# A jump, two branch hints and marker loads on TensorE's way through a decode kernel

## The chip, the cores and the metric

The kernel runs on one core of a Trainium2 chip. The time is device microseconds of one execution; the numbers given for a kernel are the median of several runs, with the lowest and the highest. The engines are named as in the profile: PE (TensorE matmuls), PEld (TensorE's weight loads), DVE (VectorE), ACT (ScalarE), POOL (GpSimd) and SP (SyncE), and beside them 16 DMA engines that move data between HBM and the on-chip memory.

## What is computed

One token (a row `x` of 1024) goes through a layer norm, and then through an attention block over a cached window and an MLP, side by side; both are added to `x`. Cut to what matters:

```python
def _A_ref(x, k_cache, v_cache, wq, wo):        # Hq 32, Hkv 4, Sk 65536, Dh 128
    W = min(4096, max(256, Sk // 4))            # 4096 last positions
    q = (x @ wq).reshape(B, Sq, Hq, Dh).transpose(0, 2, 1, 3)
    k = jnp.repeat(k_cache[:, :, Sk - W:, :], rep, axis=1)
    v = jnp.repeat(v_cache[:, :, Sk - W:, :], rep, axis=1)
    p = _softmax(jnp.einsum("bhqd,bhkd->bhqk", q, k) * (Dh ** -0.5))
    o = jnp.einsum("bhqk,bhkd->bhqd", p, v)
    return o.transpose(0, 2, 1, 3).reshape(B, Sq, Hq * Dh) @ wo

def _B_ref(x, w1, b1, w2, b2):                  # D 1024, F 3584
    h = _gelu(_layernorm(x) @ w1 + b1)
    return h @ w2 + b2

xn = _layernorm(x)
return x + _A_ref(xn, k_cache, v_cache, wq, wo) + _B_ref(xn, w1, b1, w2, b2)
```

All tensors are bfloat16.

## The kernel before

The kernel is written engine by engine, with every order and every semaphore set by hand. Nearly all of its traffic is weights and cache, each byte of which is used once.

**The loads.** SP issues all large loads on one queue, in this order: W1 (line 158, `load_rows`), the first four of each partition's eight rows of Wq (line 158), the other four (lines 229 and 230), two K loads and two V loads (line 237, `load_cache`), W2 (line 158) and Wo in four chunks of 20, 10, 1 and 1 rows (line 158, `WO_CHUNKS`). W2 is loaded into the place of W1, and Wo into that of Wq, so W2 is issued after the W1 matmuls (`C["h"]`) and Wo after the Wq matmuls (`C["q"]`); V waits for the bias matmuls (`C["b1"]`), whose row lies where V goes. ACT issues three small loads at the start: the row `x`, `b1` and `b2`.

**The detour of part of Wq.** A partition `p` holds the rows `8p` to `8p+7` of Wq. The last 1024 columns (`CUT`) of the last row of each odd partition aren't loaded into their place. Line 229 loads the even partitions whole, line 230 the odd ones without those 2 KB, and line 233 loads the 64 missing pieces with four DMAs of 16 rows into `WX`, a corner of `Pb` that is needed only later. The hole in `WA` and `WX` are set to zero first by POOL (lines 169 and 170), for which SP waits (`C["hole"]`). The q row is then made of the matmuls of line 345, which use a masked copy `XNZ7` of the normed x for the cut columns, and of four further matmuls (line 354) on `WX` with `XEZ`. `XPR`, `XEZ`, `XNZ7` and `EVEN` serve only this.

**The work on PE, in order.** The row `x` is turned into a column (lines 262 and 266), the sums for two layer norms are made (275 and 299), the bias row is put into PSUM (315). Then come the W1 matmuls (324), the Wq matmuls (345 and 354), 128 transposes of K (405), the scores (431), the transposes of the MLP's row (438), a few small matmuls for the softmax, P times V (510), and the output rows, which gather W2 (494), and after the attention's row is normed, Wo (494). Five matmuls with unused results (543, `KEEP_BUSY`) stand behind the first chunk of Wo. ACT copies the result (547), SP stores it.

**The instructions of PE.** They lie in one straight run, with no branch. Each matmul is a weight load and a matmul instruction, 763 of each in the profile. They aren't all on the engine at the start: in the trace a DMA queue of its own, q8, brings blocks of 16 KB during the run.

Of the kernel before, what the change touches and what calls it, by code (L numbers as in the profile page):

```python
# [5 lines left out]
ALU = mybir.AluOpType  # L6
ACTF = mybir.ActivationFunctionType
AX = mybir.AxisListType
# [11 lines left out]
KC = D // 128  # L20
NQ = HQ * DH
WQ_CHUNKS = [4, 4]
W1_CHUNKS = [8]
W2_CHUNKS = [28]
WO_CHUNKS = [20, 10, 1, 1]
KEEP_BUSY = [[512] * 5, [], [], []]
NPAIR = HKV // 2
PB = 2 * NBLK
CUT = 1024
B1W = 256  # L30
B1N = F // B1W
XS = 2
XROWS = 48
# [16 lines left out]
def bass_parallel_sum__sliding_block_cached__mixer_channel_mlp__decode_kernel(  # L50
# [22 lines left out]

    s_xrow, s_b1, s_b2, s_out = (nc.alloc_semaphore(n) for n in ("s_xrow", "s_b1", "s_b2", "s_out"))
    s_wq = sems("s_wq", len(WQ_CHUNKS))
    s_ex = nc.alloc_semaphore("s_ex")
# [11 lines left out]
    def sb(name, shape, d):  # L88
        return nc.alloc_sbuf_tensor(name, shape, d)
# [16 lines left out]
    EVEN = sb("EVEN", [128, 1], f32)  # L106
    XNZ7 = sb("XNZ7", [128, 15], bf16)
    XPR = sb("XPR", [1, XS * XROWS], bf16)
    XEZ = sb("XEZ", [XROWS, XS * 15], bf16)
# [28 lines left out]
    WX = Pb[0:XROWS, 0:XS * CUT]  # L138
# [7 lines left out]
    wq_runs = A_wq.rearrange("(p r) n -> p (r n)", r=KC)  # L146
    wq_x = A_wq.rearrange("(s h r e k) n -> k s h e r n", s=XS, h=2, r=4, e=4)[2 * KC - 1]
# [4 lines left out]

    C = {}

# [13 lines left out]

    POOL.mark(pool.memset(WA[:, KC * NQ - CUT:KC * NQ], 0.0))
    C["hole"] = POOL.mark(pool.memset(WX, 0.0))  # L170
    POOL.mark(pool.memset(XPR[:, :], 0.0))
# [7 lines left out]
    pool.wait_ge(s_xrow, 16)  # L179
    for i in range(XS):  # L180
        at = i * 2 * 16 * 2 * KC
        dst = XPR[0:1, i * XROWS:(i + 1) * XROWS].rearrange("o (g m) -> o g m", g=3)[:, 0:3:2, :]
        C["xpr"] = POOL.mark(pool.tensor_copy(
            dst.rearrange("o h (e r) -> o h e r", e=4),
            XBR[0:1, at + 2 * KC - 1:at + 2 * 16 * 2 * KC:2 * KC].rearrange("o (h r e) -> o h e r", h=2, e=4)))
# [5 lines left out]
    POOL.mark(pool.memset(XNZ[:, :], 0.0))  # L191
    POOL.mark(pool.memset(XNZ7[:, :], 0.0))
    C["xnz"] = POOL.mark(pool.memset(XEZ[:, :], 0.0))
# [32 lines left out]
    load_rows(WA, wq_p, WQ_CHUNKS[:-1], NQ, s_wq)  # L226
    sp.wait_ge(POOL.sem, C["hole"])
    c0 = (KC - WQ_CHUNKS[-1]) * NQ
    sp.dma_start(WA[0:128:2, c0:KC * NQ], wq_runs[0:128:2, c0:KC * NQ]).then_inc(s_wq[-1], 16)
    sp.dma_start(WA[1:128:2, c0:KC * NQ - CUT], wq_runs[1:128:2, c0:KC * NQ - CUT]).then_inc(s_wq[-1], 16)  # L230
    for i in range(XS):
        for h in range(2):
            sp.dma_start(WX[32 * h:32 * h + 16, i * CUT:(i + 1) * CUT], wq_x[i, h, :, :, NQ - CUT:NQ]).then_inc(s_ex, 16)

# [22 lines left out]

    xt = PS[:, 7 * 512 + 16: 7 * 512 + 24]
# [4 lines left out]
    xe = PS[0:XROWS, 7 * 512 + 24: 7 * 512 + 24 + XS]  # L263
    pe.wait_ge(POOL.sem, C["xpr"])
    for i in range(XS):
        last = pe.matmul(xe[:, i:i + 1], lhsT=XPR[0:1, i * XROWS:(i + 1) * XROWS], rhs=oneb[0:1, :])
# [17 lines left out]
                               op0=ALU.subtract, op1=ALU.mult))  # L284
    dve.wait_ge(POOL.sem, C["xnz"])
    DVE.mark(dve.tensor_scalar(out=XEZ[:, 7:XS * 15:15], in0=xe, scalar1=msx[0:XROWS, 2:3], scalar2=msx[0:XROWS, 7:8],
                               op0=ALU.subtract, op1=ALU.mult))
    C["even"] = DVE.mark(dve.tensor_reduce(out=EVEN[:, 0:1], in_=identf[:, 0:128:2], axis=AX.X, op=ALU.add))
    dve.wait_ge(DVE.sem, DVE.cnt)
    C["xn"] = DVE.mark(dve.tensor_copy(XNTb[:, :], XNT[:, :]))  # L290
    pool.wait_ge(DVE.sem, C["xn"])
    C["xnz7"] = POOL.mark(pool.tensor_tensor(out=XNZ7[:, 7:8], in0=XNTb[:, KC - 1:KC], in1=EVEN[:, 0:1], op=ALU.mult))
# [12 lines left out]
    ACT.mark(act.activation(out=EXPW[:, 0:1], in_=msy[:, 6:7], func=ACTF.Exp))  # L305
    dve.wait_ge(ACT.sem, C["std2"])
# [12 lines left out]
    k = 0  # L319
    for j, n in enumerate(W1_CHUNKS):  # L320
        pe.wait_ge(s_w1[j], 16)
        for _ in range(n):
            for t in range(7):
                last = pe.matmul(  # L324
                    PS[0:1, t * 512:(t + 1) * 512], lhsT=YTb[:, k:k + 1],
                    rhs=W1[:, k * F + t * 512: k * F + (t + 1) * 512],
                    start=False, stop=(k == KC - 1))
            k += 1
# [7 lines left out]
    k = 0  # L336
    for j, n in enumerate(WQ_CHUNKS):
        pe.wait_ge(s_wq[j], 16 if j < len(WQ_CHUNKS) - 1 else 32)
        for _ in range(n):
            for t in range(8):  # L340
                cut = k == KC - 1 and (t + 1) * 512 > NQ - CUT
                if cut:
                    pe.wait_ge(POOL.sem, C["xnz7"])
                z = XNZ7[:, 7 - t:15 - t] if cut else XNZ[:, 15 * k + 7 - t:15 * k + 15 - t]
                pe.matmul(  # L345
                    PS[0:8, 7 * 512:8 * 512], lhsT=z,
                    rhs=WA[:, k * NQ + t * 512: k * NQ + (t + 1) * 512],
                    start=(k == 0 and t == 0), stop=False)
            k += 1
    pe.wait_ge(s_ex, 32 * XS)  # L350
    for i in range(XS):
        for t in range((NQ - CUT) // 512, 8):
            at = i * CUT + t * 512 - (NQ - CUT)
            last = pe.matmul(  # L354
                PS[0:8, 7 * 512:8 * 512], lhsT=XEZ[:, 15 * i + 7 - t:15 * i + 15 - t], rhs=WX[:, at:at + 512],
                start=False, stop=(i == XS - 1 and t == 7))
# [34 lines left out]
    for u in range(NUNIT):  # L391
        banks = KPAIRS[u % 3]
        if u == 2:
            turn_q()
        if u == 0:
            pe.wait_ge(ACT.sem, C["a_hrow"])
            pe.wait_ge(DVE.sem, C["d_hrow"])
        if u >= 3:
            wait_kt(pe, u - 3)
        if u % 4 == 0:  # L400
            pe.wait_ge(s_k[u // 4], 16)
        col = u * 2048
        for bb in range(16):
            o = banks[bb // 8] * 1024 + (bb % 8) * 128
            last = pe.matmul(PSb[:, o:o + 128], lhsT=KT[:, col + bb * 128: col + (bb + 1) * 128],  # L405
                             rhs=identb[:, :], is_transpose=True)
        C["ktr"][u] = PE.mark(last)
        use_act = u not in (2, 5)
        dve.wait_ge(PE.sem, C["ktr"][u])
        for s in range(1 if use_act else 2):  # L410
            bk = banks[s]
            C["dkt"][u] = DVE.mark(dve.tensor_copy(  # L412
                KT[:, col + 1024 * s: col + 1024 * (s + 1)], PSb[:, bk * 1024:(bk + 1) * 1024]))
        if use_act:
            bk = banks[1]
            act.wait_ge(PE.sem, C["ktr"][u])
            C["akt"][u] = ACT.mark(act.activation(  # L417
                out=KT[:, col + 1024: col + 2048], in_=PSb[:, bk * 1024:(bk + 1) * 1024], func=ACTF.Copy))
# [7 lines left out]
    for i in range(NPAIR):  # L426
        for b in range(PB):
            if i == NPAIR - 1 and b == 3 * PB // 4:
                wait_kt(pe, 7)
            o = b * HQ + i * 2 * REP  # L430
            last = pe.matmul(  # L431
                PS[:, o:o + 2 * REP], lhsT=KT[:, (i * PB + b) * 128:(i * PB + b + 1) * 128],
                rhs=QT[:, i * 2 * REP:(i + 1) * 2 * REP],
                start=False, stop=(i == NPAIR - 1 and b % 16 == 15))
    C["sc"] = PE.mark(last)
    pe.wait_ge(DVE.sem, C["d_QT"])
    for c in range(FC):
        last = pe.matmul(PSb[:, 7 * 1024 + 2 * c: 7 * 1024 + 2 * c + 1], lhsT=Hrow[0:1, c:F:FC],
                         rhs=identb[0:1, 0:1], is_transpose=True)
    C["hT"] = PE.mark(last)  # L440
# [28 lines left out]
    C["d_T"] = DVE.mark(dve.tensor_tensor(out=U2[:, :], in0=U2[:, :], in1=HT[:, :], op=ALU.mult))  # L469
    act.wait_ge(DVE.sem, C["se"])  # L470
# [18 lines left out]
    def out_rows_mms(weights, vec, chunks, semaphores, j, stop_at=None):  # L489
        c0 = sum(chunks[:j])  # L490
        pe.wait_ge(semaphores[j], 16)
        for c in range(c0, c0 + chunks[j]):
            for a in range(4):
                ins = pe.matmul(acc(a), lhsT=vec[:, c:c + 32],  # L494
                                rhs=weights[:, c * D + a * 256: c * D + (a + 1) * 256],
                                start=False, stop=(c == stop_at))
        return ins
# [11 lines left out]
    for b in range(PB):  # L509
        last = pe.matmul(PS[0:32, 4 * 512:4 * 512 + NPAIR * DH], lhsT=Pb[:, b * HQ:(b + 1) * HQ], rhs=V4[:, :, b, :],  # L510
                         start=(b == 0), stop=(b == PB - 1))
    C["pv"] = PE.mark(last)
# [68 lines left out]
```

## The time and the profile before

| what | value |
|---|---|
| time, median of 3 runs (lowest to highest) | 100.59 us (100.56 to 101.07) |
| span of the profiled execution | 99.4 us (the page's rounding; 99.35 in the trace) |
| time less span | 1.24 us |
| busy: PE, PEld, DVE, ACT, POOL | 69.6, 42.4, 25.8, 12.8, 9.0 us |
| SP's queue q1: packets, moved, share of 16 engines' span | 1832, 39.85 MB, 94.1% |
| instruction queue q8: packets, moved | 6, 0.10 MB |
| ACT's queue q10: packets, moved | 32, 0.01 MB |
| mean rate over the span | 402 GB/s |

The profiled execution's own time isn't listed apart from its span; the time less the span stands for what lies around it.

The page's second part cuts the span into 40 slices, with the busy share of each engine and of the DMA engines in tenths. The fourth part follows the chain of waits back from the last instruction. The timeline lists the instructions by their start, merged where they follow one another; in brackets stands how long the engine was idle before and what ended it. The third part parts the DMA traffic by queue: q1 is SP's, q10 is ACT's, q8 is TensorE's instructions.

### The profile page before, as it was taken

What the parts mean: (1) busy time and instruction counts of PE and PEld (TensorE: products, weight loads), DVE (VectorE), ACT (ScalarE), POOL (GpSimd) and SP (SyncE); (2) the same over time, 40 slices, a digit from 0 to 9 for tenths busy, and PEclk for the clock granted to TensorE, in tenths of its full rate; (3) what the DMA queues carried; (4) which work ended last, traced back from release to release, by engine and by line L of the source; (5) the groups of instructions that cost most, each with busy time, mean ns of one, the idle gap of its engine ahead of it and who ended that gap; (6) DMA issues with size and microseconds to landing.
All of it is one profiled execution on the core that took longest, in us unless ns stands there. A gap on an engine that the chain in (4) does not pass through costs nothing.

```text
span 99.4 us, 1681 instructions
## 1 busy us (share of the span) xinstructions
PE 69.6 (70%) x763; PEld 42.4 (43%) x763; DVE 25.8 (26%) x50; ACT 12.8 (13%) x15; POOL 9.0 (9%) x30
## 2 busy tenths in 40 slices
PE   0230860089999999999999999722799995009961
PEld 0220300023434343434399869510567894008740
DVE  0058500000000090000078921867790040000000
ACT  0500240000000050000065730005200000000001
POOL 7989100000000000000000000000000000000000
PEclk9999999999999999999999999555557999855799
DMA  9988889999999999999999999998999899699930
GB/s 347 392 372 369 370 369 485 465 422 422 422 422 422 409 402 403 441 429 442 429 429 422 429 534 416 468 485 369 392 485 425 346 445 528 287 404 437 405 143 1
DMA packets 1870, 39.96 MB, mean 402 GB/s; under 512 B 244, under 2 KB 262, under 8 KB 584
## 3 DMA queue, kind: packets, MB, share of 16 engines
q1 hardware_dynamic: 1832, 39.85, 94.1%
q8 instruction: 6, 0.10, 0.4%
q10 hardware_dynamic: 32, 0.01, 0.0%
HBM read 39.86 MB, written 0.00 MB: 401 GB/s over the span
## 4 chain that ended last, share of the span: by engine, by line
DMA 65%; PE 31%; ACT 0%; SPq 0%; issue 0%
DMA WA<-in_A_wo_dram 46%; DMA W<-in_B_w_dram 19%; PE PS L324 15%; PE PS L345 14%; PE PS L494 2%; PE PS L354 1%; ACT ORow L547 0%; SPq L158 0%
## 5 line engine op out<-in xcount | busy, mean ns | idle before, releaser
L324 PE MATMUL PS<-W,YTb 128*1 128x512 bf16 x56 | 14.4, 425 | 6.2 <-DMA W<-in_B_w_dram 6.2
L345 PE MATMUL PS<-WA,XNZ 128*8 128x512 bf16 x64 | 14.0, 379 | 0.0
L324 PEld LDWEIGHTS PS<-W,YTb 128*1 128x1 bf16 x56 | 5.1, 91 | 16.0 <-issue 10.3
L510 PE MATMUL PS<-KV,Pb 128*32 128x256 bf16 x64 | 10.0, 333 | 1.2 <-ACT Pb L471 1.2
L494 PE MATMUL PS<-WA,OT 128*32 128x256 bf16 x128 | 5.6, 345 | 7.1 <-DMA WA<-in_A_wo_dram 7.1
L345 PEld LDWEIGHTS PS<-WA,XNZ 128*8 128x8 bf16 x64 | 5.6, 88 | 8.2
L510 PEld LDWEIGHTS PS<-KV,Pb 128*32 128x32 bf16 x64 | 7.4, 118 | 3.9 <-ACT Pb L471 1.7
L494 PEld LDWEIGHTS PS<-WA,OT 128*32 128x32 bf16 x128 | 4.5, 123 | 8.4 <-issue 6.3
L333 DVE CAST ROW<-PS 1x2048 bf16<-1x2048 f32 x1 | 2.3, 2279 | 22.2 <-PE PS L324 22.2
L417 ACT ACTIVATE KV<-PS 128x1024 bf16<-128x1024 bf16 x6 | 5.8, 1021 | 16.1 <-PE PS L405 16.1
L405 PE MATMUL PS<-identb,KV 128*128 128x128 bf16 x128 | 7.5, 219 | 0.0
L405 PEld LDWEIGHTS PS<-identb,KV 128*128 128x128 bf16 x128 | 7.2, 98 | 0.5 <-issue 0.4
L412 DVE COPY KV<-PS 128x1024 bf16<-128x1024 bf16 x10 | 6.4, 686 | 1.1 <-PE PS L405 1.1
L331 ACT ACTIVATE ROW<-PS 1x1536 bf16<-1x1536 f32 x1 | 1.4, 1440 | 21.2 <-PE PS L324 21.2
L359 DVE CAST Q<-PS 8x512 bf16<-8x512 f32 x1 | 0.7, 678 | 12.5 <-PE PS L354 12.5
L475 DVE TENSOR_REDUCE SUMP<-Pb 128x32 f32<-128x2048 bf16 x1 | 3.6, 3566 | 1.2 <-ACT Pb L471 1.2
L547 ACT ACTIVATE ORow<-PS 128x256 bf16<-128x256 f32 x1 | 0.4, 384 | 27.0 <-PE PS L494 27.0
L299 PE MATMUL PS<-YT,onesf 128*128 128x16 f32 x2 | 0.6, 383 | 4.2 <-DVE YT L297 4.2
L431 PEld LDWEIGHTS PS<-QT,KV 128*128 128x128 bf16 x128 | 3.3, 96 | 0.4 <-issue 0.4
L494 PE MATMUL PS<-W,GT 128*32 128x256 bf16 x112 | 3.4, 273 | 0.0
L431 PE MATMUL PS<-QT,KV 128*128 128x16 bf16 x128 | 3.4, 169 | 0.0
L442 DVE TENSOR_REDUCE MXP<-PS 128x32 f32<-128x2048 f32 x1 | 2.3, 2292 | 3.9 <-PE PS L431 3.9
(104 smaller groups left out, 48.8 us busy)
## 6 DMA issues: line engine op xcount, KB each, us to landing
W<-in_B_w_dram SPq DMA_DIRECT2D x2, 7168.0 KB, 31.0
WA<-in_A_wo_dram SPq DMA_DIRECT2D x1, 5120.0 KB, 40.0
WA<-in_A_wq_dram SPq DMA_DIRECT2D x1, 4096.0 KB, 28.6
KV<-in_A_k_cache_dram SPq DMA_DIRECT2D x2, 2048.0 KB, 40.2
KV<-in_A_v_cache_dram SPq DMA_DIRECT2D x2, 2048.0 KB, 43.6
WA<-in_A_wo_dram SPq DMA_DIRECT2D x1, 2560.0 KB, 45.7
WA<-in_A_wq_dram SPq DMA_DIRECT2D x1, 2048.0 KB, 31.2
WA<-in_A_wq_dram SPq DMA_DIRECT2D x1, 1920.0 KB, 36.7
```

The source lines that it names most:

```text
L324: last = pe.matmul(PS[0:1, t * 512:(t + 1) * 512], lhsT=YTb[:, k:k + 1], rhs=W1[:, k * F + t * 512: k * F + (t + 1) * 512], start=False, s ...
L331: C["a_hrow"] = ACT.mark(act.activation(out=Hrow[:, 0:1536], in_=PS[0:1, 0:1536], func=ACTF.Copy))
L333: C["d_hrow"] = DVE.mark(dve.tensor_copy(Hrow[:, 1536:F], PS[0:1, 1536:F]))
L345: pe.matmul(PS[0:8, 7 * 512:8 * 512], lhsT=z, rhs=WA[:, k * NQ + t * 512: k * NQ + (t + 1) * 512], start=(k == 0 and t == 0), stop=False)
L405: last = pe.matmul(PSb[:, o:o + 128], lhsT=KT[:, col + bb * 128: col + (bb + 1) * 128], rhs=identb[:, :], is_transpose=True)
L412: C["dkt"][u] = DVE.mark(dve.tensor_copy(KT[:, col + 1024 * s: col + 1024 * (s + 1)], PSb[:, bk * 1024:(bk + 1) * 1024]))
L417: C["akt"][u] = ACT.mark(act.activation(out=KT[:, col + 1024: col + 2048], in_=PSb[:, bk * 1024:(bk + 1) * 1024], func=ACTF.Copy))
L431: last = pe.matmul(PS[:, o:o + 2 * REP], lhsT=KT[:, (i * PB + b) * 128:(i * PB + b + 1) * 128], rhs=QT[:, i * 2 * REP:(i + 1) * 2 * REP], ...
L442: C["mxp"] = DVE.mark(dve.tensor_reduce(out=MXP[:, :], in_=PS[:, 0:2048].rearrange("p (b n) -> p n b", b=PB), axis=AX.X, op=ALU.max))
L475: C["sump"] = DVE.mark(dve.tensor_reduce(out=SUMP[:, :], in_=Pb[:, :].rearrange("p (b n) -> p n b", b=PB), axis=AX.X, op=ALU.add))
L494: ins = pe.matmul(acc(a), lhsT=vec[:, c:c + 32], rhs=weights[:, c * D + a * 256: c * D + (a + 1) * 256], start=False, stop=(c == stop_at))
L510: last = pe.matmul(PS[0:32, 4 * 512:4 * 512 + NPAIR * DH], lhsT=Pb[:, b * HQ:(b + 1) * HQ], rhs=V4[:, :, b, :], start=(b == 0), stop=(b == ...
```

## The change

Three things come, and one goes.

- **A jump at TensorE's start.** Its first instruction is a hint, which names a later branch and where that leads; then it jumps to `L_1`. The stub `L_1` stands far down, between two groups of K transposes: a no-op and a branch to `L_main`, behind the jump. The straight run jumps over the stub (`L_after`) when it gets there.
- **A second hint** among the score matmuls, for a branch some 90 instructions further on, to `L_main` again. That branch compares a register that holds 0 with 0 and is never taken. `count` in the loops finds the places, given by `BLOCK_AT`.
- **Marker loads.** ACT issues 15 DMAs behind its `EXPW` activation: load n moves n rows of 2n elements from `x` into a corner of `Pb`. Nothing reads them. The softmax's Exp, which writes `Pb`, waits for them.
- **The detour of Wq goes**, with the zeroing, the masked copies and the extra matmuls. Wq is loaded in two DMAs of four rows, all by `load_rows`.

TensorE's program has the same number of instructions before and after, since six matmuls and their weight loads go and the jumps, hints and labels come.

The diff, cut to its core:

```diff
+BLOCK_AT = [450, 640, 730]
-CUT = 1024
-XS = 2
-XROWS = 48
...
+    def at_block(i):
+        if i == 1:
+            pe.br("L_after")
+            nc.switch_bb("L_1", parent=None)
+            pe.nop(hint="t")
+            pe.br("L_main").branch_hint(first[0])
+            nc.switch_bb("L_after", parent=None)
+        if i == 2:
+            first.append(pe.mark_branch_hint_location())
+        if i == 3:
+            pe.br_lt(zero, 0, on_true="L_main", on_false="S_3").branch_hint(first[-1])
+            nc.switch_bb("S_3")
...
+    def count(n=2):
+        done[0] += n
+        if places and done[0] >= places[0]:
+            places.pop(0)
+            at_block(len(BLOCK_AT) - len(places))
...
-    POOL.mark(pool.memset(WA[:, KC * NQ - CUT:KC * NQ], 0.0))
-    C["hole"] = POOL.mark(pool.memset(WX, 0.0))
...
-    load_rows(WA, wq_p, WQ_CHUNKS[:-1], NQ, s_wq)
-    sp.wait_ge(POOL.sem, C["hole"])
-    c0 = (KC - WQ_CHUNKS[-1]) * NQ
-    sp.dma_start(WA[0:128:2, c0:KC * NQ], wq_runs[0:128:2, c0:KC * NQ]).then_inc(s_wq[-1], 16)
-    sp.dma_start(WA[1:128:2, c0:KC * NQ - CUT], wq_runs[1:128:2, c0:KC * NQ - CUT]).then_inc(s_wq[-1], 16)
-    for i in range(XS):
-        for h in range(2):
-            sp.dma_start(WX[32 * h:32 * h + 16, i * CUT:(i + 1) * CUT], wq_x[i, h, :, :, NQ - CUT:NQ]).then_inc(s_ex, 16)
+    load_rows(WA, wq_p, WQ_CHUNKS, NQ, s_wq)
...
+    first.append(pe.mark_branch_hint_location())
+    pe.br("L_1")
+    nc.switch_bb("L_main", parent=None)
+    pe.reg_mov(zero, 0)
...
+    for n in range(1, 16):
+        act.dma_start(Pb[64:64 + n, 32 * n:32 * n + 2 * n], A_x.rearrange("b s (k n) -> (b s k) n", n=64)[0:n, 0:2 * n]).then_inc(s_mark, 16)
...
-    pe.wait_ge(s_ex, 32 * XS)
-    for i in range(XS):
-        for t in range((NQ - CUT) // 512, 8):
-            at = i * CUT + t * 512 - (NQ - CUT)
-            last = pe.matmul(
-                PS[0:8, 7 * 512:8 * 512], lhsT=XEZ[:, 15 * i + 7 - t:15 * i + 15 - t], rhs=WX[:, at:at + 512],
-                start=False, stop=(i == XS - 1 and t == 7))
...
+    act.wait_ge(s_mark, 16 * 15)
```

## The prediction

> **What bounds the kernel now.** I read the page's DMA rows first, then the chain of waits, then the timeline of the two ends.
>
> ```profile
> span 99.4 us, 1681 instructions
> PE 69.6 (70%) x763; PEld 42.4 (43%) x763; DVE 25.8 (26%) x50; ACT 12.8 (13%) x15; POOL 9.0 (9%) x30
> ...
> DMA  9988889999999999999999999998999899699930
> ...
> q1 hardware_dynamic: 1832, 39.85, 94.1%
> q8 instruction: 6, 0.10, 0.4%
> q10 hardware_dynamic: 32, 0.01, 0.0%
> ```
>
> PE is busy for 70% of the span, but queue q1, which is SP's, keeps 16 DMA engines busy for 94% of it. The row by slices has no hole until the end. Note q8: six transfers of 0.10 MB together, which are blocks of instructions.
>
> ```profile
> 49.89 45.70 DMA WA<-in_A_wo_dram
> 95.59 0.04 issue
> 95.64 1.61 PE PS L494 x48
> 97.24 0.02 issue
> 97.26 0.38 ACT ORow L547
> ```
>
> This is the end of the chain of waits: the last load of Wo, then 48 small matmuls, one copy, the store. Of the 45.70 us almost all is queueing behind older loads.
>
> ```profile
> 89.61 4.00 PE L494 MATMUL PS<-WA,OT 128*32 128x256 bf16 x80 [6.18 <-DMA WA<-in_A_wo_dram]
> ...
> 95.64 1.57 PE L494 MATMUL PS<-WA,OT 128*32 128x256 bf16 x48 [0.96 <-DMA WA<-in_A_wo_dram]
> 96.92 0.10 PEld L494 LDWEIGHTS PS<-WA,OT 128*32 128x32 bf16 x4 [0.18 <-DMA WA<-in_A_wo_dram]
> ```
>
> In the timeline of the end PE stands idle for 6.18 us before the first Wo chunk, and again before the later ones. So PE has some 6 us to give away, and the time is set by the moment when the slowest of the 16 DMA engines is done.
>
> The page doesn't part the engines, but the trace's packet records (start, duration, size) do. Each engine is strictly serial: its next packet starts 3 to 4 ns before the recorded end of the last. So the packets join into 16 chains, each of which must follow the program's order of loads. This gives the last landing of every engine:
>
> - 7 plain engines: 94.37 to 94.85 us.
> - 4 engines that carry sixteen 2 KB packets more (the four WX loads of L233; all of them fall on the same four engines): 95.81 to 96.12 us.
> - 5 engines that carry one 16 KB instruction block each (q8 at 36.59, 56.24, 64.49, 75.15 and 85.86 us): 96.06, 96.38, 96.11, 96.21 and 96.26 us. The sixth block, at 96.75, comes after the data.
>
> So a fetch of TensorE's own code sets the end: 96.38 us. From there to the end of the span are 2.97 us of tail. The span is 99.35 us unrounded, the median of the runs 100.59; I carry the difference of 1.24 us along, so a microsecond on the last engine is a microsecond of the result.
>
> **The change, part by part.**
>
> *The WX detour goes.* Before, each engine loads four packets of 30,720 bytes (1,138 ns) for the odd partitions; after, it is 32,768 bytes (1,213 ns): 4 x 75 = +0.30 us on all 16 engines, less one 4-byte semaphore packet (9 ns): +0.29. The four WX engines lose 16 x 84 + 4 x 9 = 1.38 us, but they weren't last. The five fetch engines are, and they get only the +0.29. With it go two and four matmuls of PE, three DVE and POOL steps and two POOL memsets (2.75 us) ahead of `oneb`; none of this is on the path, since y is ready at 12.6 us and W1 lands at 20.2. SP loses its wait for POOL and four issues, but it only fills a queue that has a backlog.
>
> *Fetches that stay.* Of a fetch I take the price from its own engine: between two landings that the neighbours pass in equal time, an engine with a fetch needs 1.44 to 1.55 us more (0.93 to 1.04 us for the packet, the rest in slower neighbours). Take the fetch (about 1.5) or the WX packets (1.38) off each chain, and the engines' own ends lie from 94.37 to 94.88, mean 94.65. After the change: mean 94.95, plus 1.5 where a fetch falls. With about five engines hit, the latest should again stand near the upper end, at 96.65.
>
> *Marker loads.* Load n has n rows. In the trace of before a DMA of 14 rows leaves 14 packets, one to an engine, and one of a single row leaves one; so load n should use n engines, the lowest one all 15 times and the sixteenth never. A marker is below the 512-byte packets (25 to 27 ns) and above the 4-byte ones (9 ns), with a semaphore packet of 9 ns behind it: 18 to 36 ns, or 0.27 to 0.54 us on the first engine and near nothing on the last. The fetch engines weren't the first four: at most 11 markers, 0.20 to 0.40. I take 0.1, as for an engine in the upper half. On ACT the 15 issues cost 0.43 to 0.85 us each by its three issues of before, together 6 to 13 us:
>
> ```profile
> 12.28 0.29 DVE L309 TENSOR_SCALAR YTb<-YT,msy 128x8 bf16<-128x8 f32 x1
> ...
> 13.36 0.20 ACT L305 ACTIVATE EXPW<-msy 128x1 f32<-128x1 f32 x1
> ...
> 34.75 1.44 ACT L331 ACTIVATE ROW<-PS 1x1536 bf16<-1x1536 f32 x1 [21.18 <-PE PS L324]
> ```
>
> They stand behind EXPW, and ACT's next work waited 21.18 us for PE: covered, and uncovered only beyond 21 us. The new wait on `s_mark` ahead of the softmax's Exp (68.24 us) is long fulfilled.
>
> *The jump.* TensorE jumps into its third 16 KB block of instructions, runs a no-op and jumps back. No branch is in the trace. Below, it costs nothing (both blocks at hand); above, a fetch each way, each 1.0 us plus a wait behind a packet of W1 (57,344 bytes, 2.1 to 2.8 us): about 8 us. PE's first matmul was at 3.71 us; later PE stands idle 6.21 us for W1, and again 6.18 us for Wo. I take 4 us, hidden. On the DMA engines it adds one to three fetches in the first 8 us. The first may run before W1's first packet (1.81 us) and cost nearly nothing; the others cost 1.5 us, on engines that have no other fetch, as long as each fetch goes to another engine, which is what the five of before did.
>
> *The second hint.* It announces a branch back to the first block that is never taken: one more fetch, or the fetch of the next block comes late. From nothing to 1.5 us on one engine, and a wait of up to 4 us for PE near 75 us, before the idle 6.18. I take one fetch on an engine of its own: no price.
>
> [...] The rows show five fetches on five engines. [...]
>
> Sum: 0.29 + 0.1 = +0.39 us, 100.98: **101.0 us**.
>
> **Rivals.**
>
> 1. *One engine gets two fetches: slower.* With the stub, its way back and the second hint, the fetches beside the data rise from five towards nine. If the order of engines comes round again by then (five are known to differ, no more), an engine ends at 94.95 + 3.0 = 97.95 instead of 96.65: about 102.3. If the first of the two is the early one, half hidden before W1, about 101.5. It decides from the first doubled engine on. For it: the count rises. Against it: up to 16 engines are free. Chance 0.34.
> 2. *The fetches beside the data go away: faster.* If the early visit left later blocks in place, so that no engine has one, the end is at 94.88 + 0.29 = 95.17, 1.2 us earlier: 99.4. But one stub visits one block, and a single fetch left holds the end at 96.2 or later. Chance 0.10. [...]
> 3. *TensorE becomes the bound.* The jump's return and a late block after the wrong hint together exceed the idle 6.18 us. It takes over 7 us of stall: 101.5 to 104. Chance 0.06.
> 4. *The hints do nothing* (all at hand, no further fetch): the sum is the same +0.39, so it is part of the forecast.
>
> **How the numbers follow.** Forecast 0.50. Its own range, from the engines' spread (0.25) and the markers (0 to 0.4), is 100.6 to 101.2; 0.5% of 100.59 is 0.5 us, about what a measurement of this kernel can tell from no change, so of this 0.50, 0.37 is the same, 0.11 slower, 0.02 faster. Rival 1 (0.34) and 3 (0.06) are slower, rival 2 (0.10) faster. Slower 0.51, same 0.37, faster 0.12. The range reaches from 100.5 up to the doubled engine with markers, 102.5, and leaves out rival 2, the worst of rival 3 and some of the edges.
>
> **What would show it.** Right: q1 with the same 39.85 MB, q8 with seven to eleven blocks, one to three of them before 10 us; the 2 KB packets between Wq and K gone; the plain engines ending 0.3 us later; the last engine with one fetch, near 96.7, and the tail still 3.0 us. Wrong: an engine with two fetches; no q8 block between 30 and 90 us; PE not idle before the first Wo chunk; a gap in q1.

## The result, and the profile after

The changed kernel takes 101.09 us (median of 16 runs, 100.86 to 101.33), against 100.68 us for the kernel before, timed beside it in 16 runs. The ratio is 1.0042 with a 95% interval from 1.0033 to 1.0051: some 0.42 us slower. The profiled execution took 101.11 us; its span is 99.76 us, so 1.35 us lie around it.

From the page of the changed kernel, its first rows, the DMA busy share by slices, and the queues (packets, MB, share of 16 engines' span):

```profile
span 99.8 us, 1679 instructions
PE 68.5 (69%) x757; PEld 42.1 (42%) x757; DVE 24.2 (24%) x48; ACT 12.8 (13%) x15; POOL 5.6 (6%) x22
...
DMA  9988899899999999999999999999889699799920
...
q1 hardware_dynamic: 1736, 39.85, 93.7%
q8 instruction: 6, 0.10, 0.4%
q10 hardware_dynamic: 272, 0.02, 0.2%
```

The 39.85 MB of q1 are the same. It has 96 packets fewer: the 64 WX pieces of 2 KB and 32 semaphore packets. q10 has the 240 packets of the markers. q8 still has six blocks, which is the first surprise. TensorE's profiled instructions are 1,542 against 1,546 before, four fewer and not the same number: twelve matmuls and weight loads went, and eight branches, hints and the like came. That didn't decide the blocks, since experiment 1 below, with 1,534, has six as well.

The end of the chain of waits, in order of time:

```profile
50.80 45.23 DMA WA<-in_A_wo_dram
96.03 0.04 issue
96.07 1.55 PE PS L482 x48
97.62 0.02 issue
97.65 0.38 ACT ORow L537
```

It is the same chain, 0.4 us later. From the timeline, PE before Wo and ahead of the last matmuls:

```profile
90.05 4.46 PE L482 MATMUL PS<-WA,OT 128*32 128x256 bf16 x80 [6.67 <-DMA WA<-in_A_wo_dram]
...
96.07 1.33 PEld L482 LDWEIGHTS PS<-WA,OT 128*32 128x32 bf16 x48 [0.61 <-DMA WA<-in_A_wo_dram]
96.07 1.52 PE L482 MATMUL PS<-WA,OT 128*32 128x256 bf16 x48
```

PE again stands idle for 6.67 us before the first chunk of Wo, so it isn't the bound. Joining the packet records into 16 serial chains, as the prediction did, gives the last landing of each engine:

| engines | before | after |
|---|---|---|
| plain | 7: 94.37 to 94.85 us | 11: 94.88 to 95.41 |
| with the WX pieces | 4: 95.81 to 96.12 | none |
| with one instruction block beside the data | 5: 96.06 to 96.38 | 5: 96.51, 96.54, 96.59, 96.62, 96.77 |

The markers give the engines their numbers: in the trace load n has n packets of 4n bytes, from 1 of 4 bytes to 15 of 60, and the engine whose chain carries the last 15 - e of the loads is called e (engine 0 has all). In the changed kernel the engine of the first block is number 5. The start of each block, in us from the start of the span:

| kernel | q8 blocks |
|---|---|
| before | 36.59, 56.24, 64.49, 75.15, 85.86, 96.75 |
| after | 2.63, 56.95, 64.88, 77.04, 86.04, 97.15 |

The jump moved the first of the six from 36.59 to 2.63 us and added none.

### The profile page after: what moved, and what is told of

It is laid out like the page before. It is cut to its first block, busy times and chain, and to the rows that moved or that the text cites. A ratio compares the mean times of both kernels' runs of the same rounds, so it can differ in the third digit from the quotient of the medians.

```text
span 99.8 us, 1679 instructions
## 1 busy us (share of the span) xinstructions
PE 68.5 (69%) x757; PEld 42.1 (42%) x757; DVE 24.2 (24%) x48; ACT 12.8 (13%) x15; POOL 5.6 (6%) x22
## 3 DMA queue, kind: packets, MB, share of 16 engines
q1 hardware_dynamic: 1736, 39.85, 93.7%
## 4 chain that ended last, share of the span: by engine, by line
DMA 66%; PE 30%; ACT 0%; issue 0%; SPq 0%
DMA WA<-in_A_wo_dram 45%; DMA W<-in_B_w_dram 21%; PE PS L317 15%; PE PS L335 14%; PE PS L482 2%; ACT ORow L537 0%; SPq L173 0%
## 5 line engine op out<-in xcount | busy, mean ns | idle before, releaser
L499 PE MATMUL PS<-KV,Pb 128*32 128x256 bf16 x64 | 8.8, 310 | 1.3 <-ACT Pb L459 1.3
L262 PE MATMUL PS<-oneb,XBR 1*128 1x1 bf16 x8 | 0.6, 196 | 5.5 <-POOL OUTM L213 5.5
L308 PE MATMUL PS<-KV,oneb 1*1 1x512 bf16 x7 | 3.1, 620 | 0.5 <-DMA KV<-in_B_b_dram 0.5
```

The lines of the kernel that those rows point to most:

```text
L308: last = pe.matmul(PS[0:1, t * 512:(t + 1) * 512], lhsT=oneb[64:65, :], rhs=B1R[:, 2 * t:2 * t + 2, :], start=True, stop=False)
```

## The experiments

Ratios are to the kernel before, timed beside each changed version, with the 95% interval. Two ratios of different experiments that are 0.1 to 0.2% apart are at the edge of what their intervals can part.

### What each part of the change costs

**1. The detour alone** (`x1_detour_only`):

```diff
-BLOCK_AT = [450, 640, 730]
+BLOCK_AT = []
-    pe.br("L_1")            # with its hint and label
-    for n in range(1, 16):  # the marker loads
-        act.dma_start(Pb[64:64 + n, ...
-    act.wait_ge(s_mark, 16 * 15)
```

> The changed kernel without jump, hints and markers: of the change only the removal of the Wq detour is left. Theory (every engine loads 8 KB more, and the engines with a fetch of TensorE code are last): +0.29 us on the kernel before, so about 100.97, q8 with six blocks, the first near 36 us. Rival (the detour cost nothing, the whole +0.41 comes from jump and hints): 100.7, as before.

Measured: 1.0026 (1.0015 to 1.0037), 100.98 us. So 0.26 us of the 0.42 come from the detour's removal. The q8 blocks stand at 37.00, 55.88, 62.74, 75.54, 84.57 and 97.40 us; plain engines end at 94.75 to 95.28 us, those with a block at 96.34 to 96.93.

**2. Without the markers** (`x2_no_markers`): only the last three lines of the diff above.

> The changed kernel without the 15 marker loads and the wait for them. Theory (a marker costs 18 to 36 ns on each engine it uses, the fetch engines carry 5 to 10 of them): 0.1 to 0.2 us faster than the changed kernel, 100.9 to 101.0, the same as the removal of the detour alone. Rival (markers fit into gaps of the queue): 101.09, no difference.

Measured: 1.0024 (1.0012 to 1.0035), 101.06 us; 0.18% below the changed kernel's ratio, a difference good to some 0.15%, and no different from experiment 1.

**3. Without jump and hints** (`x3_no_jump`): only the first lines of that diff, markers kept.

> The changed kernel without jump, stub and both hints, markers kept. Theory (the jump only moves the fetch of the third block from 36 us to 2.6 us, and a fetch costs its engine 1.5 us wherever it stands): the same as the changed kernel, 101.05 to 101.15, with W1 landing 1.2 us earlier and TensorE's W1 matmuls starting near 20.4 instead of 21.9 us. Rival (the early fetch delays all that follows): 0.3 us or more faster.

Measured: 1.0038 (1.0026 to 1.0050), 101.13 us: the changed kernel's 1.0042 again, within some 0.15%. The timelines of this kernel and then of the changed one show what the jump does, at PE's first matmul and at its first W1 matmul:

```profile
2.24 0.63 PE L258 MATMUL PS<-oneb,XBR 1*128 1x1 bf16 x8 [2.24 <-DMA XBR<-in_A_x_dram]
...
20.50 2.72 PE L313 MATMUL PS<-W,YTb 128*1 128x512 bf16 x6 [7.75 <-DMA W<-in_B_w_dram]
```

```profile
5.51 0.63 PE L262 MATMUL PS<-oneb,XBR 1*128 1x1 bf16 x8 [5.51 <-POOL OUTM L213]
...
21.87 1.44 PE L317 MATMUL PS<-W,YTb 128*1 128x512 bf16 x3 [7.78 <-DMA W<-in_B_w_dram]
```

PE starts 3.3 us later and gets W1 1.4 us later. (The POOL named in the bracket is only what ended last by the profile; `oneb` was set at 0.90 us.) Nothing of it reaches the end, since PE waits for Wo later. W1 is late because the block is fetched on one of the 16 engines that bring W1, whose first W1 packet starts at 3.50 us instead of 1.8 to 2.5.

**4. The kernel before, with markers** (`x4_before_marked`):

```diff
+    for n in range(1, 16):
+        act.dma_start(Pb[64:64 + n, 32 * n:32 * n + 2 * n], A_x...[0:n, 0:2 * n]).then_inc(s_mark, 16)
...
+    act.wait_ge(s_mark, 16 * 15)
     act.wait_ge(DVE.sem, C["se"])
```

> The kernel before with the 15 marker loads added, nothing else. Theory: +0.1 to +0.2 us, 100.8 to 100.9. The markers name the engines: the four with the sixteen 2 KB packets are 0 to 3, the five with a fetch lie above them. Rival (markers are free): 100.7.

Measured: 1.0018 (1.0008 to 1.0028), 100.91 us. The markers cost about as much as on the changed kernel. The four WX engines are numbers 0 to 3, by their markers, and the first block falls on number 5, as in the changed kernel and in experiment 3. I don't give the numbers of the later blocks' engines: where two engines end within a few ns, the joining can't tell which is which.

### What an instruction block costs

**5. No blocks at all** (`x5_few_matmuls`). From experiment 1, with 64 matmuls instead of 757:

```diff
-        for _ in range(n):
-            for t in range(7):          # W1: 56 matmuls
+        for t in range(1):              # one; likewise in the other steps
```

> The kernel with only the detour removed, cut down on TensorE: 64 matmuls instead of 757 (one or a few of each step, the waits and all loads kept; the output is left incomplete). [...] Theory (the fetches of TensorE's code, 1.5 us on the engine that carries one, set the end): no q8 block before the last load has landed, the slowest engine done near 95.2 instead of 96.65, time 99.5, 1.5 us less than with the detour removed. Rival (all engines wait for the memory anyway, and the fetch only orders who is last): 100.6 or more.

From its page:

```profile
PE 18.5 (19%) x64; PEld 6.0 (6%) x64; DVE 24.6 (25%) x48; ACT 12.8 (13%) x15; POOL 5.6 (6%) x22
...
q1 hardware_dynamic: 1736, 39.85, 94.7%
q10 hardware_dynamic: 32, 0.01, 0.1%
```

There is no q8 row. All 16 engines end between 94.78 and 95.47 us, in one group. Time 99.71 us, ratio 0.9888 (0.9863 to 0.9913). From this to experiment 1 (1.0026) are 1.4%: what five fetches cost the kernel, by delaying one engine each. This kernel leaves out most of PE's work too, and the clock granted to TensorE was 1.0 in it against 0.90 in experiment 1, so a faster PE is a rival. Two numbers speak against it. The engines without a block end at the same time in both (94.75 to 95.28 us in experiment 1), and the tail from the last landing to the end of the span is no shorter (3.10 us against 2.99). What went is the group of five engines that ended up to 96.93 us. That PE's idle isn't what was saved shows also in the timeline of this kernel, where it waits even longer for the same load:

```profile
88.71 0.37 PE L452 MATMUL PS<-WA,OT 128*32 128x256 bf16 x1 [11.54 <-DMA WA<-in_A_wo_dram]
```

**6. Ten blocks in one tour** (`x6_tour`): the kernel of experiment 5, which visits ten far blocks.

```diff
+    pe.br("T_0")                                # after the bias matmuls
+    nc.switch_bb("T_back", parent=None)
...
+    for i in range(10):                         # far behind the program's end
+        ...                                     # 250 no-ops (370 the first time), jumped over
+        nc.switch_bb(f"T_{i}", parent=None)
+        pe.nop(hint="t", nofuse=True)
+        pe.br(f"T_{i + 1}" if i + 1 < 10 else "T_back")
```

> The same cut-down kernel, in which TensorE, after the bias matmuls (14 us), jumps through ten far blocks of otherwise unused no-ops, one jump each, and back. Ten fetches or more beside the data instead of none. Theory (each fetch goes to the next engine, 16 in turn): as many engines as fetches are 1.5 us late, none twice; the end is that of one fetch, 101.0. Rival 1 of the prediction (the order comes round after 8): some engine has two fetches, 102.3 to 102.6. If the jumps are so slow that W2 or Wo is issued late, a gap in q1 near 57 or 74 us shows it.

Measured: 115.8 us, ratio 1.1471. The time says nothing on the theories, since the tour took from 13 to 71 us and held up W2's issue. The page's DMA row has the gap that this makes:

```profile
DMA  9779779899899899999960000978979999989950
...
q8 instruction: 13, 0.21, 0.8%
```

A visit costs PE about 6 us, far more than the 0.9 to 1.1 us of the block's packet. Up to the gap the chains can be read: eight blocks (13.35 to 55.62 us) on eight different engines, which end V at 59.9 to 60.3 us, the other eight at 58.2 to 58.7.

**7. Two shorter tours** (`x7_two_tours`): five far blocks after the bias matmuls, five after P times V.

```diff
-        pe.br(f"T_{i + 1}" if i + 1 < 10 else "T_back")
+        pe.br(f"T_{i + 1}" if i + 1 not in (5, 10) else f"T_back{i + 1}")
...
+    pe.br("T_5")                                # after the rows' normalisation is started
+    nc.switch_bb("T_back10", parent=None)
     pe.wait_ge(DVE.sem, C["d_GT"])
```

> The cut-down kernel again, with two shorter tours of five far blocks each: one after the bias matmuls (12 us), one after P times V, so that neither holds up the issue of W2 or Wo (six microseconds a visit, by the long tour). Ten fetches beside the data. Theory (16 engines in turn): ten chains with one fetch each, slowest end near 96.7, time about 101. Rival (the order comes round after eight): the ninth and tenth fetch fall on engines that have one, slowest end 98, time 102.3 or more.

Ten blocks stood beside the data (15.35 to 44.47, six; 73.35 to 91.87, four). By chains: eight engines without a block end at 94.84 to 95.28 us, six with one at 96.38 to 96.68, and two with two at 97.96 and 98.51. In the joined chains the ninth and the tenth block fall on the engines of the first two. The theory of 16 engines in turn falls; the order comes round after eight. The time, 106.11 us in a single execution, is again that of the tour, which let PE go only at 100.8 us.

**8. The jump without hints** (`x8_jump_no_hints`):

```diff
-    first.append(pe.mark_branch_hint_location())
     pe.br("L_1")
...
-            pe.br("L_main").branch_hint(first[0])
+            pe.br("L_main")
...
-BLOCK_AT = [450, 640, 730]
+BLOCK_AT = [450]
```

> The changed kernel with jump and stub, without both hints and the branch that is never taken. Theory (both hints name the first block, which is still at hand, so they fetch nothing): six q8 blocks at the times of the changed kernel, the first before 3 us, TensorE's first matmul at 5.5 us, time 101.09. Rival 1 (the hint held back a fetch of the fourth block behind the jump): a second early q8 block, and none near 57 us. Rival 2 (the hint kept the first block at hand): two or three early blocks and the first matmul several us later.

Measured: 1.0033 (1.0011 to 1.0055), 101.08 us, the same within the intervals. Its six blocks stand at 1.78, 8.84, 65.07, 75.71, 86.03 and 96.97 us. None stands near 56.95, where the changed kernel has its second, and one stands at 8.84, as rival 1 of this run had it. That the two are the same block is my reading: the records give times of blocks and not their numbers. So the first hint had an effect, only not on the time: there are still five engines with one block each. The second hint lies far behind 8.84 us; of it no effect is seen, but no run leaves out that one alone.

### What the detour of Wq was worth, and why

**9. A plain split** (`x9_four_engines`), on the kernel of experiment 1:

```diff
+    wq_four = A_wq.rearrange("(a b r) n -> a b r n", a=4, r=KC)[:, :, KC - 1, NQ - CUT:NQ]   # CUT = 512
+    sp.dma_start(WA[:, c0:KC * NQ - CUT], wq_runs[:, c0:KC * NQ - CUT]).then_inc(s_wq[-1], 16)
+    sp.dma_start(WA[:, KC * NQ - CUT:KC * NQ], wq_four).then_inc(s_wq[-1], 16)
```

> The kernel with only the detour removed, but with the last 512 columns of each partition's last Wq row in a DMA of its own, straight into their place, its source written as 4 x 32 rows so that it should run on the four lowest engines. It moves as many bytes from all engines to four of them as the detour of before, without zeroing, masks or further matmuls. Theory (the detour worked only by what each DMA engine has to move): q1 with 128 packets of 1 KB on four engines, the fetch engines 0.30 us earlier, time as before, 100.6 to 100.75. Rival (the detour's gain was elsewhere): 100.97, as with the detour removed.

Measured: 1.0027 (1.0011 to 1.0043), as with the detour removed. The run doesn't test the theory: the 128 packets of 1 KB ran on all 16 engines, eight each, since 4 x 32 rows at even steps are 128 rows.

**10 and 11. Splits by the number of rows** (`x10_four_engines`, `x11_five_engines`):

```diff
+    for a, b in ((0, ROWS), (ROWS, 128)):       # ROWS, CUT = 124, 512 and 125, 640
+        sp.dma_start(WA[a:b, c1:KC * NQ], wq_runs[a:b, c1:KC * NQ]).then_inc(s_wq[-1], 16)
```

> A second try at the split, since the 4 x 32 rows were joined to 128 and ran on all engines. The last 512 columns now come in two DMAs of 124 and 4 rows. Both numbers have 4 as their largest divisor up to 16, so both should run on four engines (a DMA of 14 rows ran on 14). Theory (only what each engine has to move counts): four engines with 32 packets of 1 KB, the others 0.30 us earlier, time as before, 0.2 to 0.3% below the kernel with only the detour removed. Rival (the detour's gain lay elsewhere): no gain over 1.0026 of before.

> The same with 640 columns, in two DMAs of 125 and 3 rows, so on five engines and three. Every engine has 0.38 us less of Wq, five have about 1.45 us more, the fetch engines end 0.08 us earlier than with the detour of before. Theory: 0.998 to 1.000 of before, the fastest version so far if the fifth engine never has a fetch. Rival (it has one): two kinds of delay on one engine, 1 us slower than before.

Measured: 1.0067 (1.0054 to 1.0080) and 1.0056 (1.0037 to 1.0075). Both are slower than with no split at all. The packets of the first ran on four engines, 32 each, as meant, but took 64 ns in the mean instead of 46 (experiment 9), and 44 of the first 128 K packets, which other engines move at that time, took over 650 ns, up to 1,224. In the kernel before and in experiment 1 none of these does; nearly all take 611.

**12. The detour to other partitions** (`x12_other_rows`), one line of the kernel before:

```diff
-            sp.dma_start(WX[32 * h:32 * h + 16, i * CUT:(i + 1) * CUT], wq_x[i, h, ...
+            sp.dma_start(Pb[64 + 32 * h:80 + 32 * h, i * CUT:(i + 1) * CUT], wq_x[i, h, ...
```

> The kernel before with one edit: the four WX loads land in partitions 64 to 79 and 96 to 111 instead of 0 to 15 and 32 to 47 (the matmuls on WX read zeros, so the q row lacks these 64 pieces). Same bytes, same rows of memory, same four engines. [...] Rival (the failed splits were slow because of small packets or their number): 84 and 611 ns, time as before.

Measured: 1.0139 (1.0112 to 1.0167), 102.20 us, where the rival had the time of before. The 2 KB packets take 84 to 193 ns, 138 in the mean, instead of 84 each, and 40 of the first 128 K packets take over 650 ns. Bytes, rows of memory and engines are those of before; only the partitions written differ. So the detour's odd layout (16 rows at partition 0 and 16 at 32) was part of what made it pay: on other partitions the same detour costs 1.4%.

## Why the prediction was right

Forecast 101.0 us, +0.39 us on before; measured 101.09, +0.42% or 0.42 us. By the forecast's own bound of 0.5% this is "the same", to which it gave 0.37. It gave slower 0.51, mostly for a doubled engine, which didn't come. Part of the hit was luck. The forecast let the fetches beside the data rise towards nine, and held them to be free as long as each had an engine of its own. By experiment 7 the ninth wouldn't have had one, and rival 1's doubled engine would have come, at about 102 us. The kernel escaped that because the count was wrong as well: it stayed at five. Point by point:

- **What sets the end: right.** The slowest engine was forecast at 96.65 us plus 0.1 for markers; it was at 96.77. The tail was to stay 3.0 us; it was 2.99. Experiment 5 shows the cause: with the fetches gone, all engines end by 95.47 us (forecast for that case: 95.17) and the kernel gains 1.4%.
- **The detour, +0.29: right.** +0.26% (0.15 to 0.37) by itself. The 0.30 us of it are four packets of 1,213 instead of 1,138 ns on each engine.
- **The markers, +0.1 (0 to 0.4): somewhat more.** 0.18% (0.08 to 0.28) by experiment 4, where they are the only change; the differences of 0.12% (experiments 3 less 1) and 0.18% (changed kernel less 2) agree, and are each uncertain by some 0.15%. A marker packet takes 10.4 ns in the mean and its semaphore packet 9, at the low end of the forecast 18 to 36. Engine 5 carries ten of them: 0.2 us.
- **The jump, hidden: right in the sum, wrong in its parts.** Experiments 2 and 1 (1.0024 against 1.0026) leave nothing for it that their intervals could show. But I had it add one to three fetches and the second hint another, and looked for seven to eleven blocks in q8. There were six, with the jump and without: the further fetches were my estimate, and no run shows them. The early block stands for the one that would have come at 36.59 us, and as far as the count of six can tell, none was fetched twice. On the way out the branch took PE 3.94 us from 1.0 us on (L255 in the trace), while the 16 KB block came at 2.63; I had taken 4 us. On the way back it took 0.19 us (L150), and the next block came only at 56.95. PE's first matmul started at 5.51 us. (The prediction's upper bound for the jump took a W1 packet at 2.1 to 2.8 us; the trace of before has 2.1 to 3.1. Nothing hung on it.)
- **An early fetch is not free.** I held that the first might run ahead of W1 and cost nearly nothing. Its engine started W1 1.0 to 1.7 us after the others and ended at 96.62, among those with a late fetch. In experiments 2 and 8 the block even started at 1.90 and 1.78 us, before most of W1's first packets, and its engine still came to W1 only at 3.29 and 3.10. No engine with a block ends before 96.15 us in either. The price is about 1.5 us, early or late, somewhat less at best for the earliest. Experiment 7 shows it in one execution: engines with none, one and two blocks end around 95.1, 96.5 and 98.2 us.
- **Rival 1 (two fetches on one engine): not here, but real.** The order does come round, after eight (experiment 7), and the second fetch costs its engine 1.4 to 2.0 us again. By that one run I estimate that five blocks beside the data leave room for three more, and that the fourth would be the first to double.
- **Rival 2 (the fetches go): not here.** One stub moved a block (2.63 us instead of 36.59) or, without the hint, it seems two (1.78 and 8.84 us, experiment 8), and the time was the same (1.0042 and 1.0033, against 1.0038 without the jump).
- **Rival 3 (PE becomes the bound): no.** PE's start came 3.3 us later by the jump, and PE still waits 6.67 us for Wo.

## What to carry to other kernels

Where the DMA engines are the bound, ask for each of the 16 what it has to move, fetches of instructions included: the last one sets the time, and a page's mean of 94% doesn't show that 11 of them end 1.5 us earlier. To move a fetch in time saved nothing here, where other engines still had one (1.0042 against 1.0038); to have no block at all beside the data gained 1.4% (experiment 5), and less data for the engines that carry one, as the detour had it, 0.26% (experiment 1). Of a load that is steered to certain engines, measure also where it lands: with nothing but the partitions changed, the detour cost 1.4% (experiment 12).

## What the runs showed of the hardware, unexpected

- TensorE's instruction blocks went to eight different engines in turn, and the ninth and tenth to the first two again (experiment 7). The first block of an execution fell on engine 5 in the three profiles with markers where I could tell.
- A jump to a far block cost PE about 6 us beside a full DMA queue (experiment 6), for a packet of 0.9 to 1.1 us.
- With a hint ahead of the jump, the second block came at 56.95 us, without it at 8.84 (the changed kernel against experiment 8, which has no hint; experiment 2, with the hint, has 56.95 too).
- Four engines that wrote into other partitions than in the kernel before slowed themselves from 84 to 138 ns a packet and others from 611 to as much as 1,215 ns, at a cost of 1.4% (experiment 12). By its markers experiment 4 has the detour, in partitions 0 to 15 and 32 to 47, on engines 0 to 3. The runs show what the other partitions cost, not why.
